# GFNet mixing and SoLU feed-forward on one core: an output block stored in four transfers, and 49-row loads cut into 48 rows and one

## The chip, the core and the metric

The kernel runs on one core of a Trainium2 chip. The time is device microseconds of that core for one execution of the program; several executions are timed and the median is given, and one more is recorded by the hardware profiler. The five engines are named as in the profile: PE is TensorE (PEld its weight loads), DVE is VectorE, ACT is ScalarE, POOL is GpSimd and SP is SyncE. SP computes nothing here; it issues transfers (DMAs), as ACT and POOL do too, and 16 DMA engines carry them out. All arithmetic is float32.

## What is computed

Eight entries of 3136 tokens with 256 channels pass a Fourier transform along the tokens, a product with a filter and the transform back; the 25088 rows that come out pass a feed-forward layer with 1024 hidden values, whose activation is h times softmax(h), then normalized.

```python
def _attn_ref(x, filt_r, filt_i):            # x: (8, 3136, 256)
    X = np.fft.rfft(x, axis=1)
    Y = X * (filt_r + 1j * filt_i)[None, :, :]
    return np.fft.irfft(Y, n=x.shape[1], axis=1).astype(np.float32)

def _moe_ref(x, w_in, w_out, g_ln):          # x: (25088, 256), w_in: (256, 1024), w_out: (1024, 256)
    h = x @ w_in
    e = np.exp(h - np.max(h, axis=-1, keepdims=True))
    solu = h * (e / (np.sum(e, axis=-1, keepdims=True) + 1e-09))
    mu = np.mean(solu, axis=-1, keepdims=True)
    var = np.mean((solu - mu) ** 2, axis=-1, keepdims=True)
    return (((solu - mu) / np.sqrt(var + 1e-06) * g_ln) @ w_out).astype(np.float32)
```

## The kernel before

**Two pipelines in one.** The transform of length 3136 is factored as 49 x 64. For each entry e the kernel loads x, multiplies by a 49-point table (tile `pa`, L238 for entries 0 and 1, L281 for the others), stores the result to a scratch tensor in HBM (`d1`), fetches it again with rows and columns regrouped, makes the forward product (`pb`), multiplies by the filter on DVE, makes the inverse product (`pc`, L313), stores to a second scratch tensor (`d2`), fetches that back and makes the last 49-point product (`py`, L386), which lands in `y` in SBUF. The feed-forward layer reads `y` in blocks of 128 tokens. Its products are done in pairs of blocks, with seven products in place of eight: `m` is the first layer (L759), `o` the second (L895).

**One hand-written order.** Entry 0 is transformed alone, up to about 122 us. After that `step(k)` (L1004) runs for each of the 196 blocks and nine steps more (`LAG`), under a manual schedule: each engine gets its instructions in the order in which `step` issues them. A pair j has an even step k = 2j and an odd one. The spectrum work of entries 1 to 7 is laid between the blocks by the table `PLAN`, which gives for each entry the steps of its eight x pieces, of its seven spectrum units and of its eight pieces back. After the last entry (from about 1205 us) the blocks go on with little beside them.

**A block's way.** ACT copies and takes the exponential (L793), DVE finishes the sums and the product (L783, L805), ACT squares (L813), DVE transposes in 32 x 32 squares into the tile `turn` (L823). `regroup(p, i)` (L826) then brings one block of the pair into the layout that the second layer needs: four transfers from SBUF to SBUF, each from 32 partitions to 32 partitions, tile `solu_t`, 8 pieces of 512 bytes to a partition. POOL builds sums of `solu_t` (`project_sums`, L864, tiles `u`, one pair later), TensorE multiplies, ACT and DVE scale the result into `ot`, and `store_out(p)` (L918) writes it out. `ot` holds 128 partitions x 2 x 256 channels. Because of the transposes, the 128 partitions of one half of `ot` are 4 runs of 32 output rows, 128 rows apart in `out`:

```python
rows = out[4 * P * g:4 * P * g + 4 * P, :].rearrange("(b a i) c -> a b i c", a=4, i=32)
```

so one store is a transfer from [128 partitions, 1 KB] to [4 runs, 32 rows, 1 KB].

**Loads of x.** For entries 2 to 7 a piece i is fetched by `fetch_quarters` (L247): tile `xs[i]` holds rows of two groups g of columns, in the partitions from 0 (g = 0) and from 64 (g = 1), 49 rows each, and two halves h with two columns each. The columns of half h = 1 run downwards in x (step -C). The partitions 49 to 63 are filled too: for g = 0 the transfer takes 64 rows, and in the last entry, where x ends, 49 rows and again the first 15. For g = 1 there are 49 rows. So a piece has 4 transfers, in the last entry 6. `difference` (L261, DVE) and `sum` (L269, POOL) read the piece as soon as it is whole, TensorE's `first_quarters` (L275) follows, and `store_quarters` (L288) sends the result to `d1` on POOL's queue.

**SP's queue.** SP issues, in this order in an even step: the four transfers of `regroup(j - 3, 0)`, the four of `regroup(j - 3, 1)`, the two stores of `store_out(p)`, and, at the end of a step, the x loads placed there by the loop at L995 (three or two steps ahead of the step that uses the piece). Each waits in the queue for its own data or buffer, and what stands behind it waits too. ACT's queue fetches `d1` and the tables, POOL's the filter, `d1` stores, `d2` stores and what comes back from them.

Of the kernel before, what the change touches and what calls it, by code (L numbers as in the profile page):

```python
# [18 lines left out]
B, S, C = 8, 3136, 256  # L19
# [4 lines left out]
N1, N2 = 49, 64  # L24
# [73 lines left out]
def kernel(  # L98
# [10 lines left out]
    nc = tc.nc  # L109
# [9 lines left out]
    rows = np.arange(P)[:, None]  # L119
# [76 lines left out]
    class Spectrum:  # L196
# [50 lines left out]
        def fetch_quarters(self, i, dma):  # L247


            self.xs[i] = out = self.pools["r"].tile([P, NCH, C], FP32, name=f"x_{self.e}_{i}", tag="r")  # L250
            xb = x[self.e]
            for g in range(2):
                for h, first, step in ((0, NCH * i + 2 * g, C), (1, N2 - 1 - NCH * i - 2 * g, -C)):

                    parts = [(64, N1)] if g else [(0, 64)] if self.e + 1 < B else [(0, N1), (N1, 64 - N1)]
                    for p, n in parts:
                        dma(out=out[p:p + n, 2 * h:2 * h + 2, :],
                            in_=bass.AP(tensor=xb.tensor, offset=xb.offset + first * C,
                                        ap=[[N2 * C, n], [step, 2], [1, C]]))

        def difference(self, i):  # L261
            rows = slice(0, 64 + N1)
# [153 lines left out]
    with ExitStack() as st:  # L416
# [50 lines left out]
        second = Spectrum(1, None, None, None)  # L467
# [154 lines left out]
        for i0, n, rows in ((0, 4, P), (4, 4, P), (8, NP - 9, P), (NP - 1, 1, NQ)):  # L622
            f, at = filters[i0]
            nc.sync.dma_start(
                out=f_dram[i0:i0 + n].rearrange("i u q k c -> (u q) i (k c)")[0:rows],
                in_=f[0:rows, at:at + n].rearrange("p i k c -> p i (k c)"))
# [89 lines left out]
    def load_de(sp, u):  # L716
# [6 lines left out]
    turns, variances, solu_ts, solu_sums, spreads, rss, pos, ots, places, regrouped = (  # L723
        {} for _ in range(10))
# [193 lines left out]
    def store_out(p):  # L918
        g, second = divmod(p, 2)

        rows = out[4 * P * g:4 * P * g + 4 * P, :].rearrange("(b a i) c -> a b i c", a=4, i=32)
        for i in range(2):
            nc.sync.dma_start(out=rows[2 * second + i], in_=ots[p][:, i, :])
        del ots[p]

    blocks = NT * B // 2
# [12 lines left out]
    for e in range(1, B):  # L939
# [5 lines left out]
        for i, t in enumerate(first_at):  # L945
            dma = nc.gpsimd.dma_start
# [17 lines left out]
        for i, t in enumerate(spectrum_at):  # L964
# [4 lines left out]
            dma = nc.sync.dma_start if e == 1 and t < 8 else nc.scalar.dma_start  # L969
# [34 lines left out]
    def step(k):  # L1004
# [28 lines left out]
        if not odd:  # L1033
# [54 lines left out]
            if p in last:  # L1088
                finish_out(p, 0, 1, (0, 1), 2)
                finish_out(p, 1, 0, (1, 0), 1)  # L1090
                store_out(p)
# [4 lines left out]
            if proj and p not in last:  # L1096
                finish_out(p, 1, 0, (1, 0), 1)
                store_out(p)
# [78 lines left out]
```

## Time and profile before

| | |
|---|---|
| Median of 3 runs | 1596.14 us (1591.15 to 1606.48) |
| The profiled execution, its own time | 1601.33 us |
| Span of the profiled execution | 1599.6 us |
| Granted TensorE clock | 0.994 |
| PE busy (x instructions) | 1551.8 us (97%), x12828 |
| DVE busy | 1250.7 us (78%), x2248 |
| POOL busy | 1169.7 us (73%), x1371 |
| ACT busy | 921.4 us (58%), x1874 |
| SP's transfers (queue q1) | 271476 packets, 170.45 MB, 40.6% of 16 engines |
| POOL's (q0) and ACT's (q10) | 98.81 MB, 21.0%; 39.53 MB, 8.2% |
| Stores on SP | x196, 128 KB each |
| Regroupings on SP | x780, 128 KB each |
| 49-row loads of x on SP | x112, 98 KB each |

A page of the profile shows one execution. Busy shares are averages over stages with different limits, and a busy PE is not a PE at its peak, since the ends of its matmuls are modelled. The chain that ended last is followed backwards from the last instruction, at each step to what released it; its shares say what the time hung on. A line of waits gives who waited, for whom, microseconds in total, times, and the longest. "SPq" is SP's queue: the time in which SP issues or waits to issue. In the rows of one line's instructions the duration is minimum/median/maximum in ns.

### The profile page before, as it was taken

The numbers are of one execution on the slowest core, as the hardware profiler recorded it, in microseconds if no ns is written. First come the engines' busy times: TensorE is split into PE (matmuls) and PEld (weight loads), VectorE is DVE, ScalarE is ACT, GpSimd is POOL, SyncE is SP. The second block draws the span as 40 slices with busy tenths as digits, with TensorE's granted clock in tenths as the row PEclk, the third lists the DMA queues.
The fourth block names the chain that finished last, engine by engine and source line by source line (L and its number), as shares of the span: only waits on it lengthen the run. The fifth ranks groups of instructions, "written<-read, shape, count | busy, mean of one in ns | idle before, by whom it ended". The sixth has DMA issues, their size and how long they took to land.

```text
span 1599.6 us, 36769 instructions
## 1 busy us (share of the span) xinstructions
PE 1551.8 (97%) x12828; PEld 1058.8 (66%) x12828; DVE 1250.7 (78%) x2248; ACT 921.4 (58%) x1874; POOL 1169.7 (73%) x1371
## 2 busy tenths in 40 slices
PE   5998999999999999999999999999999999999997
PEld 1463566666666676677666677667766777777777
DVE  1887878897987788876988789887888777777673
ACT  2246555656665656666565655666565656666663
POOL 5546886789677868796779867797766766676765
PEclk8999999999999999999999999999999999999999
DMA  9989878786987589766886679766784444343434
GB/s 266 290 282 269 247 215 236 215 217 181 255 241 222 155 229 256 211 183 178 221 231 202 166 193 251 204 189 179 215 224 132 126 133 122 103 113 94 116 105 116
DMA packets 343802, 311.13 MB, mean 195 GB/s; under 512 B 27834, under 2 KB 310099, under 8 KB 343619
## 3 DMA queue, kind: packets, MB, share of 16 engines
q1 hardware_dynamic: 271476, 170.45, 40.6%
q0 software_dynamic: 33744, 98.81, 21.0%
q10 hardware_dynamic: 38400, 39.53, 8.2%
q8 instruction: 104, 1.70, 0.5%
q14 instruction: 78, 0.64, 0.1%
HBM read 124.51 MB, written 81.40 MB: 129 GB/s over the span
## 4 chain that ended last, share of the span: by engine, by line
PE 84%; DMA 9%; DVE 2%; POOL 1%; issue 1%; SPq 1%; ACT 0%; DVEq 0%; POOLq 0%; ACTq 0%
PE m L759 35%; PE o L895 34%; DMA solu_t<-turn 4%; PE py L386 4%; PE pc L313 3%; PE pb L313 3%; PE pa L281 2%; DMA x<-in_x_dram 2%; DMA f<-in_filt_r_dram 1%; SPq L840 1%; PE idler L563 1%; PE pa L238 1%; PE py L409 1%; DMA out_dram<-ot 1%; POOL u L738 1%
## 5 line engine op out<-in xcount | busy, mean ns | idle before, releaser
L895 PEld LDWEIGHTS o<-w_out_sb,solu_t 128*128 128x128 f32 x3136 | 381.5, 192 | 50.2 <-issue 43.6
L895 PE MATMUL o<-w_out_sb,solu_t 128*128 128x128 f32 x3136 | 400.9, 276 | 3.6 <-DVE ot L915 2.9
L759 PE MATMUL m<-w_in_sb,s 128*128 128x512 f32 x784 | 399.0, 610 | 2.7 <-ACT h L769 1.8
L895 PEld LDWEIGHTS o<-w_out_sb,u 128*128 128x128 f32 x2352 | 307.1, 192 | 138.9 <-issue 106.0
L895 PE MATMUL o<-w_out_sb,u 128*128 128x128 f32 x2352 | 310.6, 275 | 2.5 <-POOL u L738 1.8
L759 PE MATMUL m<-w_in_sb,y 128*128 128x512 f32 x588 | 307.6, 606 | 1.5 <-DVE h L780 1.1
L805 DVE SCALAR_TENSOR_TENSOR h<-e,h 128x1024 f32<-128x1024 f32 x196 | 304.1, 1551 | 0.1
L769 ACT COPY h<-m 128x512 f32<-128x512 f32 x294 | 173.2, 589 | 206.5 <-PE m L759 187.0
L911 ACT ACTIVATE ot<-o,rs_t 128x128 f32<-128x128 f32 x392 | 143.6, 368 | 245.2 <-PE o L895 243.8
L738 POOL TENSOR_TENSOR u<-solu_t 128x512 f32<-128x512 f32 x98 | 135.5, 1383 | 195.6 <-DMA solu_t<-turn 133.6
L783 DVE CUSTOM_DVE_ANT_0 h<-m,h 128x512 f32<-128x512 f32 x196 | 134.2, 685 | 176.8 <-ACT h L769 103.0
L813 ACT ACTIVATE h<-h,nmu 128x1024 f32<-128x1024 f32 x196 | 225.0, 1148 | 52.0 <-DVE turn L823 51.8
L823 DVE STREAM_TRANSPOSE turn<-h 128x1024 f32<-128x1024 f32 x196 | 243.1, 1240 | 3.2
L793 ACT ACTIVATE e<-h,nmax 128x1024 f32<-128x1024 f32 x196 | 225.4, 1150 | 7.9 <-DVE h L805 6.5
L738 POOL TENSOR_TENSOR u<-solu_t,u 128x512 f32<-128x512 f32 x98 | 137.7, 1405 | 95.8 <-PE o L895 95.5
L759 PEld LDWEIGHTS m<-w_in_sb,s 128*128 128x128 f32 x784 | 128.1, 191 | 89.5 <-issue 68.9
L915 DVE SCALAR_TENSOR_TENSOR ot<-o,rs_t,ot 128x128 f32<-128x128 f32 x299 | 103.7, 347 | 98.8 <-ACT ot L911 59.0
L738 POOL TENSOR_TENSOR u<-u,solu_t 128x512 f32<-128x512 f32 x98 | 159.1, 1624 | 15.5 <-PE o L895 6.4
L759 PEld LDWEIGHTS m<-w_in_sb,y 128*128 128x128 f32 x588 | 96.6, 191 | 96.7 <-issue 46.6
L738 POOL TENSOR_TENSOR solu_t<-solu_t,solu_t 128x512 f32<-128x512 f32 x98 | 153.9, 1571 | 0.9
L738 POOL TENSOR_TENSOR s<-y 128x128 f32<-128x128 f32 x196 | 99.8, 509 | 0.5
L386 PEld LDWEIGHTS py<-wb_t,t 50*64 50x64 f32 x3584 | 57.6, 134 | 42.9 <-issue 18.7
(126 smaller groups left out, 1969.1 us busy)
## 6 DMA issues: line engine op xcount, KB each, us to landing
solu_t<-turn SPq DMA_DIRECT2D x780, 128.0 KB
out_dram<-ot SPq DMA_DIRECT2D x196, 128.0 KB
t<-d POOLq DMA_DIRECT2D x112, 200.0 KB, 7.0
d<-x POOLq DMA_DIRECT2D x100, 200.0 KB, 5.3
f<-f_dram POOLq DMA_DIRECT2D x39, 512.0 KB, 8.1
t<-d ACTq DMA_DIRECT2D x37, 512.0 KB
d<-g POOLq DMA_DIRECT2D x36, 512.0 KB, 5.1
x<-in_x_dram SPq DMA_DIRECT2D x112, 98.0 KB
```

Of the source, the lines that this page charges most:

```text
L386: nc.tensor.matmul(out=views[g][64 * h:64 * h + 64, cb, i, :], lhsT=t4[rows, i, c0:c0 + 64], rhs=wb_t[rows, 0:N1], start=True, stop=True)
L738: nc.gpsimd.tensor_tensor(out=out, in0=in0, in1=in1, op=op)
L759: nc.tensor.matmul(out=ms[j, bank], lhsT=lhsT, rhs=w_in_sb[:, w, :], start=m in (1, 2, 7), stop=True, skip_group_check=True)
L769: nc.scalar.copy(out=h_half(k, i), in_=ms[j, 0])
L783: nc.vector.tensor_tensor_reduce(out=h_half(k, i), in0=ms[j, bank], in1=h_half(*kept), scale=1.0, scalar=sofar, op0=ALU.add, op1=ALU.min, ...
L793: nc.scalar.activation(out=e, in_=hs[k], func=AFT.Exp, bias=nmaxs.pop(k)[:, 1:2], scale=-1.0, accum_out=esums[g][:, i:i + 1])
L805: nc.vector.scalar_tensor_tensor(out=solu, in0=e, scalar=SHRINK, in1=solu, op0=ALU.mult, op1=ALU.mult, accum_out=nmu)
L813: nc.scalar.activation(out=solu, in_=solu, func=AFT.Square, bias=nmu, scale=-float(DFF), accum_out=variances[g][:, i:i + 1])
L823: nc.vector.transpose(out=turns[g][:, :, i, :], in_=solus[k].rearrange("p (f j) -> p f j", j=32))
L895: nc.tensor.matmul(out=pos[p, bank], lhsT=lhs[:, f, :], rhs=w[:, f, :], start=f == 0 and (m in (1, 2, 7) or alone), stop=True, skip_group_ ...
L911: nc.scalar.activation(out=out_half(p, *to)[0], in_=pos[p, 0], func=AFT.Copy, scale=rs)
L915: nc.vector.scalar_tensor_tensor(out=ot, in0=pos[p, bank], scalar=rs, in1=out_half(p, *kept)[0], op0=ALU.mult, op1=ALU.add)
```

## The change

Two places are edited. In `fetch_quarters` the 49 rows of group g = 1 become a transfer of 48 rows and one of a single row (partition 112); the single row's transfer for h = 1 reads its two columns upwards, as one run of 2 KB, and writes them in reverse order into the tile. The loads of group g = 0 stay as they are, in the last entry its 49 and 15 rows too. In `store_out` each of the two stores of a pair of blocks becomes four, one for each run of 32 output rows.

```diff
             for g in range(2):
                 for h, first, step in ((0, NCH * i + 2 * g, C), (1, N2 - 1 - NCH * i - 2 * g, -C)):
 
-                    parts = [(64, N1)] if g else [(0, 64)] if self.e + 1 < B else [(0, N1), (N1, 64 - N1)]
+                    parts = [(64, N1 - 1), (63 + N1, 1)] if g else [(0, 64)] if self.e + 1 < B else [(0, N1), (N1, 64 - N1)]
                     for p, n in parts:
-                        dma(out=out[p:p + n, 2 * h:2 * h + 2, :],
-                            in_=bass.AP(tensor=xb.tensor, offset=xb.offset + first * C,
-                                        ap=[[N2 * C, n], [step, 2], [1, C]]))
+                        step = C - 2 * C * h
+                        start = xb.offset + first * C + max(p - 64, 0) * N2 * C
+                        to = out[p:p + n, 2 * h:2 * h + 2, :]
+                        if n == 1 and h == 1:
+                            start, step, to = start - C, C, out[p:p + n, 3:1:-1, :]
+                        dma(out=to, in_=bass.AP(tensor=xb.tensor, offset=start,
+                                                ap=[[N2 * C, n], [step, 2], [1, C]]))
...
         rows = out[4 * P * g:4 * P * g + 4 * P, :].rearrange("(b a i) c -> a b i c", a=4, i=32)
         for i in range(2):
-            nc.sync.dma_start(out=rows[2 * second + i], in_=ots[p][:, i, :])
+            for b in range(4):
+                nc.sync.dma_start(out=rows[2 * second + i, b], in_=ots[p][32 * b:32 * b + 32, i, :])
```

## The prediction

> **What bounds the kernel now.** I read the page first: the busy shares and the chain of work that ended last.
>
> ```profile
> span 1599.6 us, 36769 instructions
> ...
> PE 84%; DMA 9%; DVE 2%; POOL 1%; issue 1%; SPq 1%; ACT 0%; DVEq 0%; POOLq 0%; ACTq 0%
> ```
>
> TensorE sets the pace, but 9% of the chain is transfers. The same chain cut to 200 to 1100 us, where stores, x loads and the spectrum work of entries 2 to 7 run together, says which:
>
> ```profile
> by line: PE m L759 36.7%; PE o L895 35.9%; PE py L386 4.8%; PE pa L281 4.2%; DMA solu_t<-turn 4.1%; PE pc L313 3.2%; PE pb L313 3.2%; DMA x<-in_x_dram 2.2%; issue 1.1%; DMA out_dram<-ot 1.0%; SPq L840 0.6%; SPq L257 0.4%; DVE pi L336 0.4%;
> ```
>
> Regroupings (solu_t), x loads and stores hold 4.1 + 2.2 + 1.0 = 7.3% of 900 us, 66 us. All three go out on SP's queue. Next the waits, all engines and then SP's own queue (us in total, times, longest):
>
> ```profile
> POOL u L738 <- DMA solu_t<-turn: 133.6, 44, 8.2
> ...
> POOL u L738 <- DMA x<-in_x_dram: 33.3, 8, 8.0
> POOL u L738 <- DMA out_dram<-ot: 30.9, 17, 6.0
> ...
> DVE diff L266 <- DMA x<-in_x_dram: 12.6, 9, 2.8
> ```
>
> ```profile
> SPq L840 <- PE o L859: 200.4, 39, 9.7
> SPq L840 <- DVE turn L823: 182.7, 40, 7.0
> SPq L840 <- DMA out_dram<-ot: 46.6, 41, 3.9
> ```
>
> The last line is a limit that the code doesn't show: SP's transfers share eight semaphores in turn, so a ninth waits until the first has landed. The worst place on the chain, with start and length in us:
>
> ```profile
> 822.24 10.91 DMA solu_t<-turn
> 833.15 0.02 issue
> 833.16 0.69 SPq L257
> 833.85 0.05 issue
> 833.90 0.49 SPq L257
> 834.39 0.04 issue
> 834.43 7.17 DMA x<-in_x_dram
> ```
>
> A regrouping takes 10.91 us to land, holds a semaphore, an x load goes out only then and needs 7.17 us more; the difference of that piece, and TensorE behind it, wait. From 1205 us, with no x loads, DMA is 44% busy against 73 to 85% before, and transfers leave the chain almost wholly.
>
> **Why the transfers are late.** The trace's landing records show on how many engines a transfer lies: a store reports from 4, a 49-row load from 7, a 64-row load and a regrouping from 16. With SP's median packet times (512 B 32 ns, 1 KB 46, 2 KB 84), a pair of blocks with one x piece puts on each engine that serves all of it: regroupings 8 x 16 x 32 ns = 4.1 us; two stores 2 x 32 x 46 ns = 2.9; 64-row loads 0.70; 49-row loads 1.23; together 9.0 us. Spread over 16 engines the stores would be 0.74 and the 49-row loads 0.54, together 6.1 us. The page gives the other two large queues 21.0% and 8.2%, 4.9 us of a 16.7 us pair. So the loaded engines are 13.9/16.7 = 83% busy, and evenly spread all would be 66%. Between 130 and 500 us a store lands after a median of 8.0 us; a regrouping after 6.0, with its twelfth engine done at 4.6: four engines are late.
>
> **The change, part by part.**
>
> 1. Store, landing. Four 32-row transfers replace each of 196, so 588 more. A 32-row regrouping uses 16 engines, and I take 16 for these, with 2 packets an engine each. Twelfth engine over last is 4.6/6.0, 4.3/5.3 and 3.7/4.6 in the three thirds up to 1100 us, some 0.79. I take the 66 us on the chain down by the remaining 21%: -14 us. Bounds: nothing, if all engines are equally backed up; -32 us, the time by which pairs (from the starts of their exponentials in the timeline) exceed equal mixes of TensorE work elsewhere, such as 19.85 us for the pair from 832.8 us where 15.5 would do.
>
> 2. Loads, landing. 112 loads become 48 rows in 96 cases (the 16 at rows 0 of entry 7 stay at 49) and 96 one-row loads are added. Their gain after 200 us is in part 1. Before it, where no store runs, transfers hold 11.87, 4.47 and 4.94 us of the chain at 152 to 176 us; a tenth off is -2 us (bounds 0 and -4).
>
> 3. SP's stretched issues. The chain holds 0.6 + 0.4% of 900 us = 9 us in SP's issuing, where one regrouping took 1.86 us (at 1011.15 us) against a median of 0.626. With rings less full I take -4 (bounds +4 and -6).
>
> 4. SP's time.
>
> ```profile
> L923 SPq DMA_DIRECT2D out_dram<-ot x196: 536/597/1685, 198.8 to 1594.7; - x196
> ```
>
> No row shows a 32-row store. Low end: 312 ns for a 32-row filter load (L484) and 362 for a store of 128 contiguous rows of 1 KB (L355). High end: 626 for a 32-row regrouping and 597 for today's store. It is nearest to L355's contiguous store, with the surcharge that back-to-back filter loads show (430): 0.43, and 0.07 between issues. Eight then take 4.0 us where two take 1.4: +2.6 us a pair, between +1.6 and +4.1. A one-row load costs 0.24 (the 4-row store of L194) to 0.32, two with gaps 0.65. A 48-row load costs 0.31 to 0.42 (L535) or, by the 64-row ones, 0.55 and 0.69; I take 0.49 against 0.47 and 0.32 now, so +0.85 in all per x piece, at most +1.1. With an x piece SP issues 9.1 + 2.6 + 0.85 = 12.6 of 16.7 us; the high end is 14.3. SP's waits for TensorE and the transposes (200.4 and 182.7 us) cover it. Without that cover each pair is longer by 3.4 us, 165 us over 48 pieces.
>  What is queued behind the stores: the x loads of the piece needed a pair later, then the first regrouping of the next pair. Landing, an x load that takes about 8.2 us gains 3.0 if it gets near the 5.2 of a spread load; 3.4 - 3.0 = 0.4 us late. Only the 9 pieces for which DVE's difference waits today expose it: +4 us (bounds 0 and +9 x 2.2 = +20). The regrouping is covered by POOL's next sums, a pair later.
>
> 5. The end. The last two stores go out at 1593.67 and 1594.71 us and the second lands some 3.7 us later. Eight at 0.50 start from 1593.67 and finish issuing at 1597.7; landing as a quiet regrouping does (2.4) after the last start at 1597.2 ends at 1599.6 against 1598.4: +1.2 us (bounds -1 and +3).
>
> Sum: -14 - 2 - 4 + 4 + 1.2 = -14.8. The profiled execution took 1601.33 us (1.7 around its span), 5.2 over the median of 1596.14. So 1586.5 for that execution, and 1581.3 beside the median.
>
> The Trainium skill speaks against the change: "DMA: Bandwidth & Descriptors", section "Rules for kernel authors", wants small transfers joined and calls those under 64 KB mostly overhead, and the section on the anatomy of a DMA puts some 2.0 us of fixed time on each, for POOL's route. As an estimate from that page, 684 more transfers at 2.0 us with eight in flight would be 171 us more of SP's window, and the sum would turn into a loss unless all of it were covered. The rows say that the window is held by 5 to 8 us landings under load, against 2.4 for a quiet regrouping, so it is the load on an engine that I go by.
>
> **Rivals.**
>
> The eight-semaphore window becomes the bound (slower). Place: the x loads behind eight stores, between 245 and 1100 us. Condition: a store issue near 0.63 us and landings that don't fall. Then loads leave 4.1 + 1.1 = 5.2 us later; 1.5 us of slack (639.84 against a last landing near 638.7 us, and up to 2 in quieter pairs) and 2.5 of faster landing are taken off; 1.2 us stay exposed in some 35 of 48 pieces: +42 us, part 1 doesn't come, the others give -5: 1633. For it: eight transfers today take 8 x 0.65 = 5.2 us to issue and land in 5 to 8, so the window is already full. Against: quarter stores hold an engine for 2 x 46 ns only, and empty the ring.
>
> The loaded engines explain the whole surplus (more gain): all 32 us of part 1 go, with the rest as above: -33, so 1563. For it: transfers leave the chain once x loads end. Against: in the pair from 816 us the twelfth engine was late too (9.2 of 10.9 us), so other queues share the blame.
>
> The change doesn't do what it says, or the transfers were hidden anyway: 32 contiguous rows go to fewer engines, or TensorE's busy 97% leaves nothing to win: parts 1 to 3 vanish, +1.2 stays, 1597.
>
> **How the numbers follow.** Chances: forecast 0.42, window bound 0.27, whole surplus 0.22, nothing 0.09. The predicted time is the forecast's, 1581. The forecast's own range is 1568 to 1596; for 8 in 10 I reach to the two far rivals, 1558 to 1636. One per cent, 16 us, is about what a measurement of this kernel tells from no change. Faster by over 1% (below 1580): 0.22 and 0.19 of the forecast, 0.41. Within: 0.23 + 0.09 = 0.32. Slower: 0.27.
>
> **What would show it.** Right: 784 stores at 0.31 to 0.45 us each, reporting from 16 engines and landing in 3 to 5 us before 1100 us; the regrouping's last engine close to its twelfth; DMA's share of the chain at 7 to 8%; pairs like the one from 832.8 us near 16 us. Wrong: SP issuing 0.6 us a store, its waits for out_dram far above 46.6 us, DVE's difference waiting for x in more than 9 places, or pairs of the 616 to 666 us kind above 17 us.

## The result, and the profile after

The changed kernel took 1689.36 us (median of 4 runs, 1683.17 to 1692.13) against 1595.18 us of the kernel before in the same series: ratio 1.0558, 95% interval 1.0523 to 1.0592. It is slower by some 94 us, where 1581 and at most 1636 were predicted.

The page of the changed kernel, its span and TensorE's busy time:

```profile
span 1690.3 us, 37943 instructions
...
PE 1578.6 (93%) x12828; PEld 1075.3 (64%) x12828; DVE 1222.0 (72%) x2248; ACT 922.1 (55%) x1874; POOL 1144.6 (68%) x1371
```

The same 12828 matmuls are there. The span grew by 90.7 us: TensorE's idle time by 63.9 (from 1599.6 - 1551.8 = 47.8 to 111.7) and its busy time by 26.8 (from 1551.8). The chain of this execution can't be read, as it breaks off with 23% on TensorE. The waits, all engines (us in total, times, longest):

```profile
POOL u L742 <- DMA out_dram<-ot: 153.4, 33, 9.1
POOL u L742 <- DMA solu_t<-turn: 112.0, 41, 9.7
...
PE m L763 <- DVE nmax L787: 51.0, 17, 5.2
...
DVE diff L270 <- DMA x<-in_x_dram: 59.8, 19, 8.9
DVE diff L270 <- DMA solu_t<-turn: 32.2, 7, 6.6
```

DVE's difference waited 12.6 us for x before and waits 59.8 now; TensorE waits for DVE behind it. SP's own queue:

```profile
SPq L844 <- DMA t<-d: 82.5, 20, 9.8
SPq L928 <- DMA t<-d: 59.7, 10, 12.3
SPq L928 <- DMA solu_t<-turn: 53.1, 64, 4.5
SPq L844 <- DVE turn L827: 52.0, 18, 6.0
SPq L844 <- PE o L863: 47.6, 19, 4.2
```

The waits for TensorE and for the transposes that I had counted on as cover have shrunk from 200.4 and 182.7 us to 47.6 and 52.0. In their place SP waits for **t<-d**, the fetches of spectrum pieces that ACT issues and SP never uses. With the fetches of `de` (tables for the same pieces, ACT's too), and over all of SP's lines, these waits rise from 45 us to 196.

**One place where SP stands.** The changed kernel's timeline of SP's queue, a little after 596 us (start, length, count):

```profile
595.48 1.27 SPq L844 DMA_DIRECT2D solu_t<-turn  x2
596.85 10.86 SPq L928 DMA_DIRECT2D out_dram<-ot  x8
607.87 4.71 SPq L844 DMA_DIRECT2D solu_t<-turn  x7
```

and of ACT's:

```profile
601.97 0.37 ACTq L307 DMA_DIRECT2D t<-d  x1
602.37 0.53 ACTq L723 DMA_DIRECT2D de<-de_tbl  x1
```

Eight stores that need some 3.8 us (3.81 in the pair at 1311.42 us) take 10.86. The instruction records name the semaphore that each transfer completes on; put in the order in which the turns were given out:

```
turn        issued   semaphore
SP store 1  596.85   111
ACT t<-d    601.97   112
SP store 2  597.44   113
SP store 3  597.91   115
SP store 4  598.37   116
ACT de      602.37   107
SP store 5  599.34   109
SP store 6  599.92   110
SP store 7  600.28   111
SP store 8  607.39   112   <- goes out when t<-d has landed
```

SP's and ACT's transfers take turns on the same eight semaphores (POOL's have eight of their own). A turn is given by program order, not by when an engine gets there. ACT reached its fetch only at 601.97 us, and it took 5.4 us to land; SP's eighth store holds the turn after it and stands until 607.39, with all that is queued behind. In a later pair such stands reach TensorE. SP stood for one t<-d before a regrouping, from 623.8 to 627.0 us, and for the next before the last of six x loads, from 639.2 to 641.0; in between stores waited 1.6 and 1.1 us for SP's own transfers. The x loads leave from 636.61 us on, the last two land at 644.6 and 644.7, and the timelines of DVE and TensorE go on:

```profile
644.80 0.69 DVE L270 TENSOR_TENSOR diff<-x 113x512 f32<-113x512 f32 x1 [6.28 <-DMA x<-in_x_dram]
```

```profile
646.15 2.08 PE L763 MATMUL m<-w_in_sb,y 128*128 128x512 f32 x2 [4.43 <-DVE nmax L787]
```

Eleven of the changed kernel's 15 long gaps (below) end like this one, with DVE; the other four end with ACT's scaling into `ot`. The idle 4.43 us are not the whole price. Windows of the same stretch (PE, PEld, DVE, ACT, POOL busy, then the granted clock):

```profile
646.00:648.00 2.00, 1.84 (x2) 0.84 (x3) 1.97 (x6) 0.00 (x0) 1.92 (x4) 0.50 0.89 298
648.00:650.00 2.00, 2.00 (x13) 1.98 (x12) 2.00 (x3) 0.24 (x1) 2.00 (x4) 0.66 1.22 224
650.00:652.00 2.00, 2.00 (x30) 1.32 (x28) 1.97 (x7) 1.53 (x4) 0.10 (x1) 1.00 1.14 275
```

After the gap TensorE works at half clock for a while: two matmuls take 2.08 us where two of the same size took 1.02 at 640.70 us. In the timeline after 130 us the kernel before has one gap over 2 us between matmuls (2.7 us), the changed one 15 (60.3 us in all). Its clock records show 87 us at half clock, the kernel before's 20. As an estimate from these, 67 us more at half clock can add at most half as much, some 34 us, of busy time; the same matmuls took 26.8 us more.

From the starts of the exponentials, the pairs that lost are few: 16 pairs longer by over 2 us hold 76.8 of the 85.5 us by which the pairs grew. They can be held against SP's stands. In 45 of the 97 pairs SP stood over 2 us for fetches of ACT, in the pair itself or in the one before: these grew by 86.1 us together, and all 16 are among them. The other 52 changed by -0.6 us together; in 18 of those there are x loads and eight stores too. From pair 70 on, after the last x load and the last of ACT's fetches, all pairs together differ by 0.03 us, with eight stores or with two.

### The profile page after: what moved, and what is told of

Its sections match the earlier page's. It is cut to its first block, busy times and chain, and to the rows that moved or that the text cites. A ratio compares the mean times of both kernels' runs of the same rounds, so it can differ in the third digit from the quotient of the medians.

```text
span 1690.3 us, 37943 instructions
## 1 busy us (share of the span) xinstructions
PE 1578.6 (93%) x12828; PEld 1075.3 (64%) x12828; DVE 1222.0 (72%) x2248; ACT 922.1 (55%) x1874; POOL 1144.6 (68%) x1371
## 5 line engine op out<-in xcount | busy, mean ns | idle before, releaser
L899 PEld LDWEIGHTS o<-w_out_sb,u 128*128 128x128 f32 x2352 | 318.0, 198 | 159.6 <-issue 121.7
L899 PEld LDWEIGHTS o<-w_out_sb,solu_t 128*128 128x128 f32 x3136 | 388.0, 195 | 48.8 <-issue 43.5
L899 PE MATMUL o<-w_out_sb,solu_t 128*128 128x128 f32 x3136 | 406.8, 278 | 3.2 <-DVE ot L919 2.9
L763 PE MATMUL m<-w_in_sb,y 128*128 128x512 f32 x588 | 319.4, 627 | 54.3 <-DVE nmax L787 49.5
L899 PE MATMUL o<-w_out_sb,u 128*128 128x128 f32 x2352 | 321.1, 282 | 15.9 <-ACT ot L915 14.2
L742 POOL TENSOR_TENSOR u<-solu_t 128x512 f32<-128x512 f32 x98 | 129.7, 1323 | 266.3 <-DMA out_dram<-ot 153.4
L809 DVE SCALAR_TENSOR_TENSOR h<-e,h 128x1024 f32<-128x1024 f32 x196 | 296.0, 1510 | 0.1
L742 POOL TENSOR_TENSOR u<-solu_t,u 128x512 f32<-128x512 f32 x98 | 132.8, 1356 | 100.9 <-PE o L899 100.5
L742 POOL TENSOR_TENSOR u<-u,solu_t 128x512 f32<-128x512 f32 x98 | 152.9, 1560 | 16.6 <-PE o L899 9.8
L270 DVE TENSOR_TENSOR diff<-x 113x512 f32<-113x512 f32 x48 | 35.6, 741 | 92.8 <-DMA x<-in_x_dram 59.8
```

The source lines that it names most:

```text
L270: nc.vector.tensor_tensor(out=diff[rows], in0=xi[rows, 2:4, :], in1=xi[rows, 0:2, :], op=ALU.subtract)
L742: nc.gpsimd.tensor_tensor(out=out, in0=in0, in1=in1, op=op)
L763: nc.tensor.matmul(out=ms[j, bank], lhsT=lhsT, rhs=w_in_sb[:, w, :], start=m in (1, 2, 7), stop=True, skip_group_check=True)
L809: nc.vector.scalar_tensor_tensor(out=solu, in0=e, scalar=SHRINK, in1=solu, op0=ALU.mult, op1=ALU.mult, accum_out=nmu)
L899: nc.tensor.matmul(out=pos[p, bank], lhsT=lhs[:, f, :], rhs=w[:, f, :], start=f == 0 and (m in (1, 2, 7) or alone), stop=True, skip_group_ ...
```

## The experiments

The theory, called R in the expectations: the stores' turns bring SP round to the semaphore of a fetch of ACT that hasn't landed. Its rivals: the pieces of x (X), the time that the stores take of SP's queue (Q), the shape of the new stores (S). Each run is given as median and ratio to the kernel before in the same series.

**1. The stores alone.** The loads are left as they were.

```diff
         for i in range(2):
-            nc.sync.dma_start(out=rows[2 * second + i], in_=ots[p][:, i, :])
+            for b in range(4):
+                nc.sync.dma_start(out=rows[2 * second + i, b], in_=ots[p][32 * b:32 * b + 32, i, :])
```

> The four-way store alone, x loads as before. Theory R (ring): SP and ACT take turns on the same eight completion semaphores, eight quick stores turn the ring past an ACT fetch of d1 (t<-d) or of the table (de) that has not landed, and SP stands still until it has; most of the loss comes with the stores: 1650 to 1680 us, SP's waits for t<-d and de 120 to 180 us in total. Theory Q (queue time): the stores' own issue, 8 x 0.46 us against 2 x 0.65, puts the x loads 2.4 us later in each of 48 pieces: 1640 to 1680 us too, but with SP's waits for t<-d near the 30 us of before. Theory X (the one-row loads are the trouble): near 1596 us.

Measured: 1685.09 us, 1.0518 (1.0450 to 1.0587). SP's waits for ACT's fetches are 192 us. Time and waits both lie a little above R's ranges; the waits are far from the 30 us of Q, and X is out. The stores make nearly the whole loss, 86 of 94 us. Here too 43 pairs with such stands hold all of it (+92.0 us), and the others together changed by -3.1. Its chain is recorded almost whole, and can stand beside the 84% and 9% of before:

```profile
PE 72%; DMA 15%; DVE 4%; issue 3%; POOL 2%; SPq 2%; ACT 1%; ACTq 0%; DVEq 0%; POOLq 0%
```

**2. The pieces of x alone.** The stores are left as they were.

```diff
-                    parts = [(64, N1)] if g else [(0, 64)] if self.e + 1 < B else [(0, N1), (N1, 64 - N1)]
+                    parts = [(64, N1 - 1), (63 + N1, 1)] if g else [(0, 64)] if self.e + 1 < B else [(0, N1), (N1, 64 - N1)]
...
```

> The x split alone, stores as before. Theory R: two more turns of the ring in a pair with an x piece, not enough to overtake the fetches often: 1590 to 1612 us, SP's waits for t<-d and de under 60 us. Theory Q: 1.0 us more SP time a piece: 1596 to 1620 us. Theory X: near the changed kernel, 1670 to 1690 us.

Measured: 1609.27 us, 1.0070 (1.0047 to 1.0093); waits for ACT's fetches 38 us, no more than before. A small loss of its own, some 10 to 11 us, inside the ranges of R and Q alike.

**3 and 4. ACT's fetches issued by POOL,** in the changed kernel and, as a control, in the one before. POOL's transfers use other semaphores.

```diff
-        nc.scalar.dma_start(out=de[:, 0:pairs],
+        nc.gpsimd.dma_start(out=de[:, 0:pairs],
...
-            dma = nc.sync.dma_start if e == 1 and t < 8 else nc.scalar.dma_start
+            dma = nc.sync.dma_start if e == 1 and t < 8 else nc.gpsimd.dma_start
```

> The changed kernel with the spectrum's fetches (t<-d and de) issued by POOL instead of ACT, so that they take POOL's own eight semaphores and SP's ring holds SP's transfers alone. To be read against its control, the kernel before with the same move. Theory R: SP's waits for t<-d vanish, the pairs of 20 to 25 us with them, and the kernel stands within 15 us of its control, perhaps under it. Theory Q: the queue is as long as in the changed kernel, so it stays 60 to 95 us over its control.

> Control: the kernel before with the spectrum's fetches (t<-d and de) issued by POOL instead of ACT. No theory gives its time closely: POOL's queue gets some 90 issues of 0.6 to 0.8 us more, 60 us in all on an engine that is 73% busy, and its sums may wait behind a fetch; 1585 to 1640 us. Only the distance of the other kernel from this one counts.

Measured: 1633.17 us, 1.0199 (1.0165 to 1.0233) for the changed kernel, and 1603.70, 1.0024 (0.9998 to 1.0050) for the control. So the distance between changed and old shrinks from 94 to 29.5 us: some two thirds of the loss hang on where ACT's fetches are issued. R had expected at most 15 us to be left and Q at least 60, so neither is the whole account. SP's waits in the changed kernel with fetches on POOL:

```profile
SPq L844 <- PE o L863: 95.1, 28, 5.9
SPq L928 <- DMA solu_t<-turn: 92.7, 93, 4.5
SPq L844 <- DVE turn L827: 66.0, 23, 5.3
```

The waits for t<-d are gone from the top; half of the cover is back (SP's waits for TensorE and DVE add up to 221 us, 471 in the kernel before); stores now wait for regroupings of SP's own, a microsecond each time.

**5, 6 and 8. The x loads of a step issued ahead of its stores,** in the changed kernel, in that with fetches on POOL, and in the one before.

```diff
...
-            loads[at].append(load)
+            (x_loads if latest == t - 2 else loads)[at].append(load)
...
+                for job in x_loads[k]:
+                    job()
+                x_loads[k] = []
                 store_out(p)
...
-        for job in late[k] + loads[k]:
+        for job in late[k] + x_loads[k] + loads[k]:
```

> The changed kernel, fetches on ACT as they were, with the x loads of an even step issued on SP ahead of the eight stores. Theory R (shared ring): the stores still meet the semaphores of ACT's fetches and SP still stands for them, SP's waits for t<-d and de stay over 100 us; the regroupings behind the stores are late in place of the x loads: 1625 to 1675 us. Theory Q (queue time of the stores ahead of the x loads) alone: the loss goes, 1595 to 1612 us.

> The changed kernel with both moves: fetches on POOL, x loads ahead of the stores. Read against 1633 us (fetches on POOL alone) and 1604 us (control). If the 29 us that the move of the fetches leaves are x loads queued behind eight stores (DVE's difference waits 39 us for x there, 3 us in the control): 1600 to 1615 us, that wait under 10 us. If they are late regroupings: 1625 to 1640 us, POOL's sums still waiting over 130 us for SP's transfers.

> Control for the order: the kernel before with the x loads of an even step issued ahead of its two stores. x loads leave 1.4 us earlier, stores 2.4 us later, nothing else moves: 1585 to 1600 us under either theory.

Measured: 1719.12 us, 1.0765 (1.0738 to 1.0791); 1643.98, 1.0293 (1.0242 to 1.0344); 1606.94, 1.0047 (1.0028 to 1.0066). If x loads standing behind eight stores were the loss, putting them in front would have cured it. It made each kernel slower, the changed one by 30 us; SP's waits for ACT's fetches rose from 196 to 242 us. In run 6 DVE's wait for x did fall, from 39.2 us in run 3 to 6.9, and the time rose all the same. So Q, as x loads held up behind the stores, is out as the main cause. All three times lie above their ranges, R's for run 5 (at most 1675 us) and that of the control too. That the x loads take turns as well, and only change who stands at the bad one, would fit; no run here shows it by itself.

**7. Four stores of 64 KB.** Each serves 32 partitions with both rows of output, so it is spread like the change's stores at half the number of turns.

```diff
-        for i in range(2):
-            nc.sync.dma_start(out=rows[2 * second + i], in_=ots[p][:, i, :])
+        for b in range(4):
+            nc.sync.dma_start(out=rows[2 * second:2 * second + 2, b].rearrange("a i c -> i a c"),
+                              in_=ots[p][32 * b:32 * b + 32])
```

> The kernel before with four 64 KB stores for a pair of blocks (32 partitions x two 1 KB rows, both halves of ot in one) instead of two of 128 KB; x loads and fetches as before. 16 engines each, but two more turns of the ring instead of six. Theory R: few fetches are overtaken, SP's waits for t<-d and de 40 to 80 us, 1590 to 1615 us. Theory Q: 4 x 0.46 us against 2 x 0.65 is 0.6 us more, 1590 to 1600 us. If the four-engine store had cost what the prediction said: 1580 to 1590 us.

Measured: 1604.56 us, 1.0045 (1.0019 to 1.0071). SP's waits:

```profile
SPq L840 <- PE o L859: 155.3, 39, 8.5
SPq L840 <- DVE turn L823: 126.1, 31, 6.6
SPq L840 <- DMA t<-d: 94.2, 22, 11.0
```

The time is only 7.6 us up, inside R's range and above the other two. But R's reason missed: 40 to 80 us of waits for ACT's fetches were expected and there are 162 in all (the expectation of run 12 has 141, which leaves out some lines), not far below the changed kernel's 196. Such stands cost little here, where 281 us of cover are left in these lines.

**9 and 10. Turns without quarter stores.** The kernel before with its two whole stores, and three transfers of 64 bytes behind each, so that SP takes eight turns a pair again; in run 10 with ACT's fetches on POOL. The transfers go into a spare tile.

```diff
+    turn_rows = consts.tile([6, 16], FP32, name="turn_rows")
...
         for i in range(2):
             nc.sync.dma_start(out=rows[2 * second + i], in_=ots[p][:, i, :])
+            for k in range(3 * i, 3 * i + 3):
+                nc.sync.dma_start(out=turn_rows[k:k + 1, :], in_=x[0, k:k + 1, 0:16])
```

> The kernel before with its two whole stores for each pair, and behind each of them three added transfers of SP of 64 bytes (16 elements of a row of x into a spare tile that nothing reads). So SP issues eight transfers for a pair as the changed kernel does, but the stores' shape, bytes and engines are the old ones. Theory R (turns: SP's and ACT's transfers take turns on eight completion semaphores, and eight transfers in a row bring SP round to the semaphore of a fetch of ACT that is still on its way): the added turns alone bring most of the loss, 1655 to 1690 us, and SP's waits that end with the landings of t<-d and de rise from 42 us to 150 or more. Rival S (the 32-row shape itself, or the load of the quarter stores on all engines, makes the loss): 1596 to 1612 us, with waits for t<-d and de below 80 us. Six small issues of some 0.1 to 0.4 us each cost SP 0.6 to 2.4 us for a pair under both.

> The kernel of the run with six small transfers for a pair, and with the fetches t<-d and de issued by POOL instead of ACT. Theory R: the coupling with ACT is gone, so most of that kernel's surplus goes: 1600 to 1633 us, SP's waits for t<-d and de below 25 us. Of the remainder that the changed kernel kept with its fetches on POOL (29.5 us), this tells whether SP's own turns make it (1625 to 1635) or the quarter stores' size and queue time (1600 to 1612). Rival S: equal to the kernel before with its fetches on POOL, 1600 to 1608 us, and so is the kernel with small transfers and fetches on ACT.

Measured: 1716.59 us, 1.0710 (1.0655 to 1.0765), and 1717.97, 1.0688 (1.0608 to 1.0767). Run 9 refutes S: without any 32-row store, added transfers lose more than the change does. It isn't what R said either: the time is above its range, and SP's waits for ACT's fetches are 135 us where 150 or more were expected. Run 10 refutes R as I had put it: with ACT's fetches out of the ring, 1600 to 1633 was expected; those waits fell to 18 us, and no time came back. Its SP queue says who holds the turns there:

```profile
SPq L926 <- DMA solu_t<-turn: 109.7, 111, 4.9
...
SPq L258 <- DMA out_dram<-ot: 46.7, 39, 2.7
SPq L924 <- DMA solu_t<-turn: 44.6, 38, 4.0
SPq L841 <- DMA out_dram<-ot: 35.6, 36, 2.8
```

L926 is the small transfer, L924 the store, L258 the x load. Small transfers and stores now wait for regroupings, and x loads and regroupings for the whole stores, which land after medians of 6.9, 5.7 and 5.7 us (here and below from 130 to 500, 500 to 800 and 800 to 1100 us, from the start of the issue to the last report of the semaphore). The theory has to be wider: SP can't issue until the transfer eight turns back has landed, whosever it is.

**11. The four-way stores with ACT's fetches on POOL.** The diffs of runs 1 and 3 together: stores of the change, loads of before.

> The kernel before with the four-way stores alone (x loads as before), and the fetches t<-d and de issued by POOL. The changed kernel with fetches on POOL stood at 1633, the kernel before with fetches on POOL at 1604. If the stores make the remaining 29.5 us: 1625 to 1637 us. If the pieces of x make it (they cost 11 us by themselves, and the pairs that stay longer are those with x loads): 1604 to 1615 us. SP's waits for t<-d and de below 25 us either way.

Measured: 1632.30 us, 1.0179 (1.0122 to 1.0237), the same as with the x pieces (1633.17). So what remains beside ACT's fetches is the stores', and nothing clear of noise is left there for the x pieces. Compare it with run 10. Both take eight store turns a pair without ACT in the ring, and SP's issuing adds up to the same (1102 us in run 10, 1096 here). They are 86 us apart, and the transfers in the ring take different times to land: here 4.0, 3.2 and 2.9 us for a quarter store and 5.4, 4.7 and 4.8 for a regrouping, which takes 6.9, 5.8 and 5.2 in run 10. That fits the wider theory, but the two runs also differ in how many engines a store lies on.

**12. Four 64 KB stores with ACT's fetches on POOL.** The diffs of runs 7 and 3 together.

> The kernel before with four stores of 64 KB for each pair (32 partitions with two rows of output each) and the fetches t<-d and de issued by POOL. With fetches on ACT the four 64 KB stores stood at 1604.6 us with 141 us of SP's waits for t<-d and de, 7 us above before. Theory R: without that coupling the stores' quicker landings are left without their price, and it stands at 1590 to 1602 us, below the kernel before with fetches on POOL (1603.7). If half as many turns still cost by themselves, or the fetches on POOL cost 4 us as in the control, 1602 to 1612 us.

Measured: 1599.52 us, 0.9994 (0.9969 to 1.0019). This keeps most of the quicker landings at a third of the turns: 196 more instead of 588, stores that land after 4.9, 3.9 and 2.8 us (7.8, 5.3 and 5.9 in the control, run 4), and its SP queue is covered again:

```profile
SPq L840 <- PE o L859: 220.9, 44, 9.3
SPq L840 <- DVE turn L823: 175.1, 44, 7.1
```

Its chain, to be held against the 84% and 9% of before:

```profile
PE 87%; DMA 6%; DVE 1%; issue 1%; SPq 1%; POOL 1%; ACT 0%; POOLq 0%; DVEq 0%; ACTq 0%
```

It is level with the kernel before, not faster; no version here beats that one beyond its interval.

## Why the prediction was wrong, point by point

**The account of SP's queue.** The loss can be laid out in one account, of the trace's own figures for SP, before and after. Issuing rose from 840 to 1107 us (+267); waits for ACT's fetches from 45 to 196 (+151); waits for its own stores fell from 49 to 5; waits for TensorE and DVE, the cover, fell from 471 to 142 (-328). Most of what is then left of the 91 us is gaps of up to 0.15 us between instructions (+31). Run 7 has the rise of ACT's waits with little of the other and stays within 8 us; run 11 has the rise in issuing without the waits and pays 29. In the changed kernel both fall into the same pairs, and all of the loss stands in those. Run 10 shows that ACT's fetches aren't the only way to use up the cover.

**Part 4 failed, where SP's waits for TensorE and the transposes were to cover it.** Its prices were good: a store's issue has a median of 0.42 us where I took 0.43.

```profile
L928 SPq DMA_DIRECT2D out_dram<-ot x784: 314/420/1945, 203.4 to 1687.8; - x196
```

The 48-row loads took 0.59 and 0.33 us, the single rows 0.28 and 0.69, against 0.49 and 0.65 for two. What was missing is a term. I wrote that SP's transfers share eight semaphores in turn, and didn't look at ACT's: they take turns on the same eight. Each pair now goes six turns further round the ring, so it meets, within the eight, fetches that ACT issues late. Moving these fetches away is worth 94 - 29.5 us, some 65, by runs 3 and 4, and with the stores' other 29 the part stands near +94, where I had +4. The cover was also a total, 383 us, set against an average pair; the loss sits in 16 pairs.

**Part 1 failed in its size.** The mechanism came true: stores report from 16 engines and land after 3.2, 2.7 and 2.4 us in the three stretches (7.1, 6.2 and 5.3 before), regroupings after 4.8, 3.4 and 3.5 (5.7, 5.1 and 4.5). The landings before were somewhat quicker than the prediction has them: it took 8.0 and 6.0 us for the first stretch, and 638.7 us for a landing that the records put at 637.7. Run 12 has most of the gain in landing. Against its control, the ratios 0.9994 and 1.0024 differ by 0.3%, 5 us, and their intervals overlap; I had -14, and up to -32; no run shows a gain clear of noise. The share of the chain was the wrong measure. In run 12 transfers fell from 9% to 6% of the chain, and TensorE took over what they left. What could be won stood in another view of the kernel before, its windows (PE busy is the first engine):

```profile
200.00:1100.00 900.00, 891.39 (x8051) 612.14 (x8048) 744.94 (x1315) 540.43 (x1112) 703.23 (x831) 1.00 0.77 211
```

TensorE idled 8.6 us in these 900. So most of the 66 us of transfers on the chain ran while it did other work.

**Part 2**: -2 for the start didn't come. The first exponential is at 125.6 us instead of 122.4, and at 124.2 with the x pieces alone; but it is at 122.3 in run 3 with the x pieces and at 124.0 in run 1 without, so the +3 isn't shown to be theirs. **Part 3** had the right sign (regroupings' issue fell from 576 to 547 us in sum), and was worth nothing once SP waited. **Part 5**: +1.2 became +2.1 (from the last exponential but one to the end 40.0 us, 37.9 before).

**The rivals.** The window rival named what became the bound, and its side. Its place was wrong: the wait is at the stores and regroupings themselves (142 us of t<-d there), and x loads put first made it worse. Its condition, an issue near 0.63 us and landings that don't fall, wasn't met. Its 1633 is close to runs 3 and 11, but by another sum, and it had no term for ACT. The rival of more gain and the one of no effect are out.

**The page's rule.** "DMA: Bandwidth & Descriptors", "Rules for kernel authors", in the Trainium skill, had spoken against the change: transfers under 64 KB are mostly overhead. Here eight stores of 32 KB lose 86 us (run 1) and four of 64 KB lose 7.6 (run 7), so the rule's direction holds. A fixed price for each transfer isn't enough to explain it: with the same number of turns and the same time in issuing, runs 10 and 11 differ by 86 us.

**What stays open.** The 29 us of run 11 over run 4 (by medians of two series; by their ratios some 25) were not divided between the turns and the issuing, which rises by 243 us there. SP's waits for its own regroupings rise from 31 to 97 us, which fits the turns but doesn't prove them. Moving ACT's fetches to POOL also moves their issue in time; the control puts that at 4.5 us for the kernel before only. And why that move gives 65 us back beside quarter stores and nothing beside small transfers is only argued, from the landings.

## What to carry to other kernels

Before you split a transfer, count how often its queue will go round the ring of completion semaphores, list every transfer of other engines that takes turns on the same ring, and ask which of them lands last; the splits that lost little or nothing here are the ones that keep the number small (four of 64 KB), and none gained. Take the most that a change can win from the bounding engine's idle time in that stretch (8.6 us here), not from the share that transfers hold of a chain. And hold a cover against the pairs where the stalls fall, not against its sum.

## What the runs showed of the hardware

Three things that I had not expected. A queue can stand for a transfer that it neither issued nor uses: up to 12.3 us at one store. A stall of TensorE costs more than its length: at each of the changed kernel's 15 gaps of over 2 us the clock records show 0.50 for 3.4 or 6.8 us, and the same matmuls took 26.8 us more of busy time, beside 63.9 more of idle time. The Trainium skill, "TensorE: Matmul & The Clock Gate", section "What's actually happening", says that an idle window of about 3.4 us halves the clock until a busy one has passed; the records' steps of 3.413 us agree, but gaps of 2.5 to 3.3 us did it here too, and in run 11 gaps of 2.1 and 2.9 us did not. And small transfers are not quick ones: 64 bytes from x took SP 0.25 us to issue and landed after 4.9, 4.1 and 4.0 us in the three stretches in run 10, no sooner than the quarter stores of 32 KB in run 11.
